# Three of four stored pairs of w_out blocks kept on chip in the ring, and the row transposes moved to the second product

## The chip, the cores and the metric

The kernel runs on one core of a Trainium2 chip. A core has TensorE (PE in the profile, with its weight loads as PEld), VectorE (DVE), ScalarE (ACT), GpSimd (POOL) and SyncE (SP), which here issues most of the DMAs. The metric is the device time of one launch in microseconds, the median of several runs.

## The reference

Attention over a window of 128 positions feeds a mixture of eight experts, and its result feeds one wide feed-forward layer:

```python
    scores = np.where(mask, scores + bias[None], -1000000000.0)
    attn = np.exp(scores - np.max(scores, axis=-1, keepdims=True)); attn = attn / (np.sum(attn, ...) + 1e-09)
    x = np.matmul(attn, v)             # (4, 8, 576, 64) -> 2304 rows of 512
    ...
    expert_idx = np.argmax(x @ w_gate, axis=1)
    for e in range(E):                 # 8 experts, w1[e] 512x1024, w2[e] 1024x512
        xe = x[expert_idx == e]
        h = np.maximum(xe @ w1[e], 0.0)
        out[mask] = gate_w[mask, None] * (h @ w2[e])
    ...
    r = np.maximum(x @ w_in, 0.0)      # w_in 512x2048
    return (r * r) @ w_out             # w_out 2048x512
```

(The softmax is drawn together here, and x is the output of the stage before in each case.)

## The kernel before

The program has three stages. Attention and the routing fill the first 183 us or so; the eight experts run from there to about 405 us; the wide layer, called moe2 here, takes the rest. Nearly all products are in float16 with each operand split into a high and a low half, so that one product is three matmuls.

**An expert.** The routed rows of expert e are fetched by row number (`gather_x`, L778) into tiles `xg`, turned by eight transposes of 128 columns each on PE (`transpose_x`, L786, into the PSUM tile `ps_d`), and copied to SBUF by ACT (L787). `turn` does this for one block of 128 rows. Expert e has two or three blocks. `s1` then computes one eighth of h per call: twelve matmuls (L795 to L797, four groups of three) into `ps_a` or `ps_b`, two buffers each, and the relu on ACT (L798, high half) and DVE (L799, low half). `s2` multiplies h by w2 into four PSUM tiles `c, c, a, b` (L849 to L851), so its fourth needs a buffer of `ps_b` that the relu of the step fc = 5 of `s1` gives back. At the end of `s2` ACT copies the result to `yT` (L854), which frees `ps_a` for the third step, fc = 2, of the next expert's `s1`.

**Weights.** Each expert has four tiles of w1 and four of w2. `load_w` brings one in two steps: SP loads 512 KB of float32 (L747) into a raw tile, and `split` writes the high half on ACT (L769) and the low half on DVE (L770) into a tile of the ring `wr`, which has 12 tiles of 128x2048 float16. Raw tiles come from the pool `rw` (four tiles) and, from expert 2 on, partly from the unused `wi` tiles.

**The wide weights.** w_in and w_out come as 64-bit words. While the experts run, `wide()` does one decoding step at a time: SP loads the words into a tile of `rw` (L866), DVE turns them into float32 in the single tile `dec` (L871, L872, L873), and when `wide()` is called the next time, the `finish` of the step splits `dec` (L918 on ACT and L919 on DVE for w_out, L902 and L903 for w_in). The list `STEPS` says after which steps of which expert it is called. The first eight steps decode the blocks of w_out called `SENT`, four pairs: they have no place on chip yet, so `finish` puts them into unused parts of four `wi` tiles, SP stores them to DRAM (`wod`, L922), and `fetch_out` brings the four pairs back into the four tiles of `rw` when moe2 begins (L960). Then come 16 steps for w_in, and eight for the blocks `KEPT`, which go to four ring tiles.

**Order.** Every engine runs its instructions in the order that a scheduler settled when the kernel was built, from the order of the code and from the buffers. A tile of the ring is given to its next user when its last reader is done, and a split for a tile not yet free waits in ACT's queue with all that stands behind it.

**moe2.** For each group G of rows and half m, `seven` makes the squared activations in a list `g` of ring tiles, two for G < 3 and four from G = 3 on; the products with w_out read the four pairs of `KEPT` and the four of `SENT`.

## Time and profile before

| | before |
|---|---|
| median of 3 runs | 749.85 us (747.07 to 750.89) |
| profiled execution | 754.0 us |
| its span, first to last instruction | 752.2 us |
| mean granted TensorE clock | 0.988 of full speed |
| PE busy | 711.6 us, 95% of the span |
| DVE busy | 594.4 us, 79% |
| ACT busy | 442.9 us, 59% |
| stores of w_out blocks to DRAM | 8 of 256 KB |
| fetches of them | 4 of 512 KB |

The profiled execution is one run; its time is its span and 1.8 us around it. The busy time of an engine is the sum of its instructions' times; the waits of PE are listed by the instruction that waited and what it waited for.

### The profile page before, as it was taken

The page shows a single profiled execution, that of the slowest core. Times are in us where ns is not written, and L with a number is a line of the kernel's source. Part 1 is how long each engine was busy: PE and PEld are TensorE (multiplying, and loading weights), DVE is VectorE, ACT ScalarE, POOL GpSimd, SP SyncE. Part 2 cuts the span into 40 slices and gives each one's busy share as a digit, 9 for nine tenths or more (in the row PEclk, how much of TensorE's full clock was granted, in tenths as well). Part 3 has the DMA queues.
Part 4 walks back from the last instruction along what each step waited for, and adds up shares of the span by engine and source line. Part 5 has one row for each costly group of instructions (what it writes and reads, how often), then busy time and mean ns, then how long its engine had stood idle before and what let it go on. Part 6 is the DMA issues. An engine that isn't in the chain of part 4 may idle for free. (4 is left out here: it accounts for less than half of the span.)

```text
span 752.2 us, 19605 instructions
## 1 busy us (share of the span) xinstructions
PE 711.6 (95%) x7979; PEld 600.8 (80%) x7979; DVE 594.4 (79%) x1454; ACT 442.9 (59%) x748; POOL 212.0 (28%) x247
## 2 busy tenths in 40 slices
PE   5989899999988999999899999999999999999996
PEld 5889799788755666788798566777899999999995
DVE  5888788864788999969987987868678787878672
ACT  5878788852466655657544342435657575757561
POOL 4493522335353401000000346533411111111011
PEclk9999999989999999999999999999999999999998
DMA  8798203765899887467713000000000000000000
GB/s 329 289 379 186 80 30 53 294 152 178 221 300 319 281 264 233 131 212 239 233 48 127 17 16 15 2 30 1 30 2 30 2 30 2 30 2 30 2 30 29
DMA packets 35656, 91.71 MB, mean 122 GB/s; under 512 B 5209, under 2 KB 13547, under 8 KB 35547
## 3 DMA queue, kind: packets, MB, share of 16 engines
q1 hardware_dynamic: 29803, 75.77, 31.6%
q0 software_dynamic: 5760, 14.65, 5.9%
q8 instruction: 64, 1.05, 0.6%
q14 instruction: 29, 0.24, 0.1%
HBM read 77.54 MB, written 13.04 MB: 120 GB/s over the span
## 5 line engine op out<-in xcount | busy, mean ns | idle before, releaser
L1178 PEld LDWEIGHTS <-wi 128*128 128x128 f16 x3024 | 170.6, 98 | 4.3 <-issue 3.1
L1315 PEld LDWEIGHTS <-wr 128*128 128x128 f16 x1008 | 98.1, 98 | 12.1 <-issue 0.7
L1201 ACT CAST wr<-work 128x1024 f16<-128x1024 f32 (+1 forms) x72 | 59.9, 832 | 58.3 <-DVE work L1207 41.6
L1178 PE MATMUL ps_a<-work,wi 128*128 128x128 f16 x1344 | 84.2, 219 | 0.0
L1178 PE MATMUL ps_b<-work,wi 128*128 128x128 f16 x1272 | 79.7, 219 | 0.4 <-ACTq L1066 0.4
L1202 DVE TENSOR_TENSOR wr<-work,wr 128x1024 f16<-128x1024 f32 (+1 forms) x72 | 70.3, 1000 | 4.4 <-ACT wr L1201 4.4
L310 PE MATMUL ps_a<-yT,wr 128*128 128x192 f32 (+2 forms) x288 | 64.9, 346 | 6.9 <-DMA wr<-in_q_dram 4.8
L322 ACT ACTIVATE pb<-pb,nm 128x192 f32<-128x192 f32 (+2 forms) x144 | 56.1, 433 | 14.8 <-DVE nm L315 14.1
L1343 POOL DMA_INDIRECT out_dram<-o,oid x18 | 25.6, 1423 | 101.4 <-ACT o L1341 66.8
L769 ACT ACTIVATE wr<-rw 128x1024 f16<-128x1024 f32 x40 | 42.2, 1057 | 19.5 <-DMA rw<-in_w_dram 18.9
L1278 POOL TENSOR_TENSOR yT<-wr 128x512 f32<-128x512 f16 x8 | 11.2, 1401 | 148.3 <-ACTq L1066 117.1
L310 PEld LDWEIGHTS ps_a<-yT,wr 128*128 128x128 f32 x288 | 45.6, 200 | 8.2 <-DMA yT<-in_k_dram 7.0
L315 DVE CUSTOM_DVE_ANT_0 pb<-ps_a,bias 128x192 f32<-128x192 f32 (+2 forms) x144 | 44.1, 326 | 9.9 <-PE ps_a L310 7.8
L770 DVE SCALAR_TENSOR_TENSOR wr<-rw,wr 128x1024 f16<-128x1024 f32 x40 | 48.8, 1220 | 3.6 <-ACT wr L769 3.4
L1210 ACT ACTIVATE work<-work 128x1024 f32<-128x1024 f32 x24 | 25.4, 1058 | 37.7 <-DVE work L1198 37.7
L333 PE MATMUL ps_b<-cst,pb 128*128 128x128 f32 x256 | 43.9, 283 | 0.7 <-ACT pts L337 0.7
L795 PE MATMUL ps_a<-work,wr 128*128 128x352 f16 (+4 forms) x112 | 33.7, 301 | 5.4 <-ACT yT L854 3.9
L778 POOL DMA_INDIRECT xg<-xd,idx x21 | 25.8, 1227 | 36.8 <-PE ps_d L786 27.7
L849 PE MATMUL ps_c<-work,wr 128*128 128x352 f16 (+5 forms) x128 | 35.9, 283 | 0.3 <-DVE work L1198 0.3
L851 PE MATMUL ps_c<-work,wr 128*128 128x352 f16 (+5 forms) x128 | 35.9, 283 | 0.0
L850 PE MATMUL ps_c<-work,wr 128*128 128x352 f16 (+5 forms) x128 | 35.9, 283 | 0.0
L1227 DVE TENSOR_TENSOR work<-work 128x512 f32<-128x512 f32 x18 | 13.0, 725 | 28.7 <-ACT work L1195 28.7
(308 smaller groups left out, 2009.5 us busy)
## 6 DMA issues: line engine op xcount, KB each, us to landing
rw<-in_w_dram SPq DMA_DIRECT2D x40, 512.0 KB
wi<-in_w_dram SPq DMA_DIRECT2D x20, 512.0 KB
rw<-in_wo_dram SPq DMA_DIRECT2D x16, 512.0 KB
rw<-in_wi_dram SPq DMA_DIRECT2D x32, 256.0 KB
wr<-in_q_dram SPq DMA_DIRECT2D x14, 512.0 KB
xd<-xhl POOLq DMA_DIRECT2D x16, 256.0 KB
yT<-in_k_dram SPq DMA_DIRECT2D x7, 576.0 KB
rw<-in_v_dram SPq DMA_DIRECT2D x12, 325.0 KB
```

The lines of the kernel that those rows point to most:

```text
L310: nc.tensor.matmul(ps[:, s, first:hi], q[g, u, hh // 4][:, hh % 4, s if u < 4 else 0, :], self.kt[g, hh // 2][:, hh % 2, key0:key0 + hi - ...
L315: self.last_ttr = nc.vector.tensor_tensor_reduce(out=pb[:, s, first:hi], in0=ps[:, s, first:hi], in1=self.bias[:, hh, first - lo:192], sca ...
L322: self.last_exp = nc.scalar.activation(pb[:, s, first:hi], pb[:, s, first:hi], AF.Exp, bias=nm[:, s:s + 1], scale=-1.0)
L333: nc.tensor.transpose(pt[:, t, :, s, :], pb[:, s, t * P:(t + 1) * P], self.idf)
L769: self.nc.scalar.activation(t[:, 0], st, AF.Copy, scale=sc)
L770: self.nc.vector.scalar_tensor_tensor(t[:, 1], st, sc, t[:, 0], op0=ALU.mult, op1=ALU.subtract)
L849: nc.tensor.matmul(py, wh, hh, start=fc == 0, stop=False)
L850: nc.tensor.matmul(py, wl, hh, start=False, stop=False)
L1178: self.nc.tensor.matmul(ps[:, j], w[:, kp, a, w0 * P:(w0 + 1) * P], v[:, 2 * x + kp], start=kp + b == 0, stop=kp == 1 and b == 2)
L1201: self.end_act = self.fin_act = nc.scalar.copy(hi, src)
L1202: self.end_dve = self.fin_dve = V.tensor_tensor(lo, src, hi, op=ALU.subtract)
L1315: nc.tensor.matmul(ps[n], x[:, v, j], y[j][:, w], start=m + i + j == 0, stop=m == 1 and i == 2 and j == 3)
```

## The change

`SENT` is cut to one pair. The other three pairs, now called `HELD`, get three ring tiles of their own when they are decoded (`wo_tiles` at the head of `out_step`), and `finish` writes straight into them. These tiles are never given back, so nine of the twelve ring tiles are left for the experts. Six of the eight stores are gone, and `fetch_out` brings one pair instead of four, so three of the four `rw` tiles are free in moe2; there the first half of each group from G = 3 on takes three of its four `g` tiles from `rw`. Independently, the transposes of the next expert's rows, which stood after the steps 3, 5 and 7 of `s1`, stand for every expert but the first inside `s2`, after its steps 1, 3 and 5, ahead of the load of a w2 tile. PE has the same instructions in number as before. In the changed file lines stand one further down up to `out_step`, four in it, and more behind it: L769 is L770, L918 is L922.

```diff
--- before.py
+++ after.py
@@ -54,7 +54,8 @@
          ((1, 3, 5, 7), (1, 3)))
 SPARE = ((), (), (4, 5, 6, 7), (4, 5, 6, 7), (4, 5, 6, 7), (6, 7), (7,), ())
 KEPT = (0, 1, 8, 9, 2, 3, 10, 11)
-SENT = (4, 5, 12, 13, 6, 7, 14, 15)
+HELD = (4, 5, 12, 13, 6, 7)
+SENT = (14, 15)
 
 C_REL, C_ID, C_LT, C_IOTA, C_J, C_TOK, C_ROWS = 0, 192, 320, 448, 457, 477, 495
 NC_CONST = 503
@@ -907,17 +908,20 @@
     def out_step(self, fc):
 
         nc = self.nc
+        if fc in HELD and fc not in self.wo_s:
+            for _ in self.wo_tiles((fc, fc + 1), lambda: self.ring(F16, [P, 2048])):
+                pass
         f = self.wide_load(self.wo, [(slice(fc * P, (fc + 1) * P), lambda r, k: r, DM, lambda st, k: st)])
 
         def finish():
-            if fc in KEPT:
+            if fc not in SENT:
                 dst = self.wo_s[fc]
             else:
                 dst = self.wi_s[4 + SENT.index(fc) % 4].rearrange("p k a c -> p (k a c)")[:, 2048:3072].rearrange(
                     "p (a d) -> p a d", a=2)
             nc.scalar.activation(dst[:, 0], f, AF.Copy, scale=WOSC)
             nc.vector.scalar_tensor_tensor(dst[:, 1], f, WOSC, dst[:, 0], op0=ALU.mult, op1=ALU.subtract)
-            if fc not in KEPT:
+            if fc in SENT:
                 o = SENT.index(fc) * 2 * DM
                 self.stored.append(lambda: nc.sync.dma_start(self.wod[:, o:o + 2 * DM],
                                                              dst.rearrange("p a d -> p (a d)")))
@@ -943,7 +947,7 @@
         self.wi_s = [wp.tile([P, 2, 2, 7 * P], F16, name=f"wi{k}", tag=f"wi{k}") for k in range(8)]
         self.wo_s, self.wo_pair = {}, {}
         self.stored, self.finish = [], None
-        self.steps = [(self.out_step, fc) for fc in SENT] + \
+        self.steps = [(self.out_step, fc) for fc in HELD + SENT] + \
             [(self.in_step, fp, kp) for fp in range(8) for kp in range(2)] + [(self.out_step, fc) for fc in KEPT]
 
     def wo_tiles(self, fcs, make):
@@ -1026,12 +1030,14 @@
                     w[1, e + 1, fc // 2] = self.load_w(1, e + 1, fc // 2)
                 if fc in STEPS[e][0]:
                     wide()
-                if fc in (3, 5, 7) and more:
+                if fc in (3, 5, 7) and e == 0:
                     turn(nxt, e + 1, fc // 2 - 1)
                 if e == 7 and fc == 1:
                     next(nrm)
 
             def then(d):
+                if more and e > 0 and d < 3:
+                    turn(nxt, e + 1, d)
                 if more:
                     w[2, e + 1, d] = self.load_w(2, e + 1, d)
                 if e + 2 < E:
@@ -1189,7 +1195,9 @@
         u, p5, z, p1 = (self.part(22528 + 2048 * k, 4 * P).rearrange("p (j n) -> p j n", j=4) for k in range(4))
         mul = lambda *a: self.product(G, m, *a)
         n = 2 if G < SG else 4
-        g = self.gts[G, m] = [self.ring(F16, [P, 2, 8 * P]) for _ in range(n)]
+        spare = 3 if n == 4 and m == 0 else 0
+        g = self.gts[G, m] = [self.ring(F16, [P, 2, 8 * P]) for _ in range(n - spare)] + \
+            [self.rw.tile([P, 2048], F16, tag="rw", name="rw").rearrange("p (a n) -> p a n", a=2) for _ in range(spare)]
 
         def keep(dst, ps):
             self.fin_act = nc.scalar.activation(dst, ps, AF.Copy, scale=RSC)
```

Three places of the order are shown, with the buffers' numbers. The first is ACT in `s1` of expert 0, where the first two decoded blocks are finished (`dec` is the decoded block, `work` the relu's result or the turned rows, `wi4` and `wi5` the old places of the blocks, `wr` a ring tile). Before:

```order
L787 COPY work_3335<-ps_d_3685 128x8x128
L918 ACTIVATE wi4_3343<-dec_3334 128x512
L817 ACTIVATE work_3335<-ps_a_3649 128x128
L817 ACTIVATE work_3335<-ps_b_3656 128x128
L817 ACTIVATE work_3335<-ps_a_3663 128x128
L817 ACTIVATE work_3335<-ps_b_3678 128x128
L918 ACTIVATE wi5_3344<-dec_3334 128x512
```

After:

```order
L788 COPY work_3335<-ps_d_3685 128x8x128
L818 ACTIVATE work_3335<-ps_a_3650 128x128
L922 ACTIVATE wr_3405<-dec_3334 128x512
L818 ACTIVATE work_3335<-ps_b_3657 128x128
L818 ACTIVATE work_3335<-ps_a_3664 128x128
L818 ACTIVATE work_3335<-ps_b_3678 128x128
L818 ACTIVATE work_3335<-ps_a_3695 128x128
L818 ACTIVATE work_3335<-ps_b_3702 128x128
L922 ACTIVATE wr_3405<-dec_3334 128x512
```

The first finish moved behind the relu of step 0 and the second behind that of step 5; before they stood ahead of step 0 and behind step 3.

The second is DVE in `s1` of expert 1, round the relu of step fc = 5, whose input is `ps_b_3994` before and `ps_b_3981` after. L770 (L771 after) with `rw` as its source is a weight split; `wr_3917` and `wr_3916` are the first tile of w1 of expert 2, `wr_3966` and `wr_3963` the second. Before:

```order
L770 SCALAR_TENSOR_TENSOR wr_3880<-rw_3878,wr_3880 128x1024
L770 SCALAR_TENSOR_TENSOR wr_3917<-rw_3915,wr_3917 128x1024
L919 SCALAR_TENSOR_TENSOR wi7_3346<-dec_3334,wi7_3346 128x512
L799 SCALAR_TENSOR_TENSOR work_3335<-ps_a_3979,work_3335 128x384
L770 SCALAR_TENSOR_TENSOR wr_3966<-wi4_3343,wr_3966 128x1024
L871 TENSOR_SCALAR dec_3334<-rw_3925 128x512
L799 SCALAR_TENSOR_TENSOR work_3335<-ps_b_3994,work_3335 128x384
```

After:

```order
L771 SCALAR_TENSOR_TENSOR wr_3879<-rw_3877,wr_3879 128x1024
L771 SCALAR_TENSOR_TENSOR wr_3916<-rw_3914,wr_3916 128x1024
L923 SCALAR_TENSOR_TENSOR wi5_3344<-dec_3334,wi5_3344 128x512
L800 SCALAR_TENSOR_TENSOR work_3335<-ps_b_3981,work_3335 128x384
L771 SCALAR_TENSOR_TENSOR wr_3963<-wi4_3343,wr_3963 128x1024
L872 TENSOR_SCALAR dec_3334<-rw_3922 128x512
L800 SCALAR_TENSOR_TENSOR work_3335<-ps_a_4014,work_3335 128x384
```

The relu of step 5 moved ahead of the split of expert 2's second tile; the split of the first tile and a finish still stand ahead of it.

The third is ACT at the end of `s2` of expert 1 and the start of `s1` of expert 2 (`yT` is the result of `s2`; the sources of the splits are raw tiles). Before:

```order
L769 ACTIVATE wr_4181<-rw_4179 128x1024
L769 ACTIVATE wr_4220<-wi7_3346 128x1024
L902 ACTIVATE wi0_3339<-dec_3334 128x896
L769 ACTIVATE wr_4303<-rw_4301 128x1024
L769 ACTIVATE wr_4337<-wi4_3343 128x1024
L854 COPY yT_75<-ps_c_4081 128x384
L854 COPY yT_75<-ps_c_4082 128x384
L854 COPY yT_75<-ps_a_4083 128x384
L854 COPY yT_75<-ps_b_4084 128x384
L769 ACTIVATE wr_4394<-rw_4392 128x1024
L798 ACTIVATE work_3335<-ps_a_4271 128x352
```

After:

```order
L770 ACTIVATE wr_4178<-rw_4176 128x1024
L788 COPY work_3335<-ps_d_4166 128x8x96
L770 ACTIVATE wr_4217<-wi7_3346 128x1024
L903 ACTIVATE wi0_3339<-dec_3334 128x896
L855 COPY yT_75<-ps_c_4048 128x384
L855 COPY yT_75<-ps_c_4049 128x384
L855 COPY yT_75<-ps_a_4050 128x384
L855 COPY yT_75<-ps_b_4051 128x384
L770 ACTIVATE wr_4300<-rw_4298 128x1024
L799 ACTIVATE work_3335<-ps_a_4268 128x352
```

The splits `wr_4303` and `wr_4337` of expert 3's first two tiles stood ahead of the copies to `yT`; now (`wr_4300` and the next) they stand behind them. The copy of the last turned block is new ahead of them, and the split of expert 2's last w2 tile (`wr_4220`, now `wr_4217`) stands ahead of them in both.

## Rows read from the trace of the kernel before

**Rows 1.** The page's first part: busy time, share of the span, instructions of each engine.

```profile
PE 711.6 (95%) x7979; PEld 600.8 (80%) x7979; DVE 594.4 (79%) x1454; ACT 442.9 (59%) x748; POOL 212.0 (28%) x247
```

**Rows 2.** Waits of PE, 155 to 405 us: what waited, for whom, total, times, longest.

```profile
PE ps_a L795 <- ACT yT L854: 3.9, 3, 2.1
PE ps_d L786 <- DMA xg<-xd,idx: 3.4, 1, 3.4
```

**Rows 3.** Stretches: length, busy of PE, PEld, DVE, ACT, POOL; PEclk, DMA share, GB/s.

```profile
208.10:211.50 3.40, 3.17 (x16) 1.96 (x17) 3.36 (x6) 2.30 (x5) 0.67 (x2) 0.50 0.96 296
242.20:245.60 3.40, 3.40 (x14) 1.72 (x13) 3.40 (x12) 3.26 (x5) 1.65 (x2) 0.50 0.74 215
...
205.00:215.00 10.00, 6.67 (x43) 4.22 (x44) 8.28 (x13) 5.83 (x8) 6.15 (x8) 0.83 0.90 295
...
356.80:378.70 21.90, 19.18 (x187) 17.09 (x187) 20.89 (x43) 12.08 (x23) 0.00 (x0) 1.00 0.70 221
378.70:413.00 34.30, 33.36 (x470) 32.55 (x468) 27.91 (x51) 14.26 (x27) 1.16 (x1) 1.00 0.24 81
...
450.00:752.20 302.20, 293.67 (x3763) 258.54 (x3760) 224.76 (x355) 166.36 (x225) 78.41 (x69) 0.99 0.05 17
```

**Rows 4.** PE in time, experts 1 to 3: start, length, line, [idle before <- releaser].

```profile
208.34 1.03 PE L786 MATMUL ps_d<-id,xg 128*128 128x128 f16 x8 [3.35 <-DMA xg<-xd,idx]
...
214.22 0.61 PE L786 MATMUL ps_d<-id,xg 128*128 128x128 f16 x8
...
218.56 0.51 PE L786 MATMUL ps_d<-id,xg 96*128 96x96 f16 x8
...
221.55 0.32 PE L849 MATMUL ps_b<-work,wr 128*128 128x384 f16 x1 [1.02 <-DVE work L799]
...
235.69 0.31 PE L795 MATMUL ps_a<-work,wr 128*128 128x352 f16 x1
...
241.55 0.31 PE L795 MATMUL ps_a<-work,wr 128*128 128x352 f16 x1 [2.12 <-ACT yT L854]
...
274.75 0.31 PE L795 MATMUL ps_a<-work,wr 128*128 128x352 f16 x1 [1.48 <-ACT yT L854]
```

**Rows 5.** DVE in time, end of s1 of expert 1.

```profile
217.86 0.68 DVE L919 SCALAR_TENSOR_TENSOR wi<-dec,wi 128x512 f16<-128x512 f32 x1
...
219.47 1.23 DVE L770 SCALAR_TENSOR_TENSOR wr<-wi,wr 128x1024 f16<-128x1024 f32 x1 [0.46 <-ACT wr L769]
...
220.95 0.55 DVE L799 SCALAR_TENSOR_TENSOR work<-ps_b,work 128x384 f16<-128x384 f32 x1
```

**Rows 6.** ACT in time, s1 of expert 0, s1 of expert 1, start of s1 of expert 2.

```profile
184.20 0.64 ACT L918 ACTIVATE wi<-dec 128x512 f16<-128x512 f32 x1
...
185.55 0.28 ACT L817 ACTIVATE work<-ps_b 128x128 f16<-128x128 f32 x1 [0.54 <-PE ps_b L816]
...
187.73 0.63 ACT L918 ACTIVATE wi<-dec 128x512 f16<-128x512 f32 x1
...
189.14 0.27 ACT L817 ACTIVATE work<-ps_b 128x128 f16<-128x128 f32 x1
...
215.62 1.06 ACT L769 ACTIVATE wr<-rw 128x1024 f16<-128x1024 f32 x1 [0.62 <-DMA rw<-in_w_dram]
...
239.33 1.04 ACT L769 ACTIVATE wr<-wi 128x1024 f16<-128x1024 f32 x1
240.28 0.84 ACT L854 COPY yT<-ps_c 128x384 f32 x2
```

**Rows 7.** SP in time: DMA issues.

```profile
209.39 0.33 SPq L747 DMA_DIRECT2D rw<-in_w_dram  x1
```

**Rows 8.** Groups of instructions, 155 to 405 us: count | busy, mean ns | idle before, releasers.

```profile
L769 ACT ACTIVATE wr<-rw 128x1024 f16<-128x1024 f32 x36 | 38.0, 1057 | 19.5 <-DMA rw<-in_w_dram 18.9 <-PE ps_b L851 0.5
L872 DVE SCALAR_TENSOR_TENSOR dec<-rw,dec 128x512 uint32<-128x512 uint32 x31 | 21.4, 689 | 0.6
L871 DVE TENSOR_SCALAR dec<-rw 128x512 uint32<-128x512 uint32 x31 | 13.4, 433 | 9.2 <-PE ps_b L851 7.9 <-DMA rw<-in_wi_dram 0.7
```

## The prediction

> **What bounds the kernel now.** I read the page's busy times first: PE is busy 95% of the span [rows 1], so what can be won is its idle time, 752.2 - 711.6 = 40.6 us in all, and stretches in which it runs at the lower clock. The change takes no matmul away, and PE executes the same instructions in another order. Next come the list of what PE waited for between 155 and 405 us, the part in which the experts run and in which all that the change removes lies: the two largest entries are three waits for the copy to `yT`, 3.9 us together, and one of 3.4 us for gathered rows [rows 2]. Then the stretches: twice the granted clock is 0.50, the 1.2 GHz level, for 3.40 us, each time just after one of those waits [rows 3]. Work that takes 3.40 us at half clock takes 1.7 us at full clock, so each such stretch costs 1.7 us beside its wait. From 450 us on PE is busy 293.67 of 302.20 us [rows 3]; there the change only puts three of four `g` tiles elsewhere, and I count that part as unchanged. So the question is what becomes of the waits in experts 1 to 7, and whether ACT and DVE, which do the splits and the decoding, give new ones.
>
> **The wait for the gathered rows.** At 208.34 us the first transposes of expert 2's rows stand in PE's queue between two steps of `s1` and the gather has not landed: 3.35 us idle [rows 4], then the half-clock stretch to 211.50 us [rows 3]. After the change the transposes stand in the next product, some 9 us later, when the rows are there. The wait goes; it costs nothing later for other experts, whose gathers caused no wait of this kind before. The three blocks themselves (1.03, 0.61 and 0.51 us, the first at half clock, so about 1.6 us on PE at full clock) are moved and not saved.
>
> But little of the 3.35 us is a gain at once, since the next thing was late too. The fourth tile of `s2` of expert 1 needs `ps_b`, free only when DVE has done the relu of step 5; PE waited 1.02 us for it, to 221.55 us [rows 4]. That relu ran at 220.95 us, behind the split of expert 2's second w1 tile at 219.47 us and, before that, a finish that ended at 217.86 + 0.68 = 218.54 us [rows 5]. In the new order it stands ahead of the second tile's split, but still behind the first tile's split and the finish. With nothing else moved it runs at 218.54 us and `ps_b` is free at 219.1 us, 2.4 us earlier than before.
>
> Two things shift that. **Earlier:** the first tile's split waited for its load; ACT began it at 215.62 us, straight after a wait for the DMA [rows 6], and the load was issued at 209.39 us [rows 7], 6.2 us before. In 205 to 215 us the DMA engines were busy 0.90 of the time at 295 GB/s [rows 3]. Three of the six removed stores were issued at 196 to 203 us; 3 x 262 KB at 295 GB/s is 2.7 us of transfer that no longer lies ahead. (The Trainium skill, "DMA: Bandwidth & Descriptors", section "Anatomy of one DMA", gives a single transfer about 2.0 us and its bytes at 436 GB/s, some 3.2 us as an estimate for 512 KB. That section measured transfers issued from GpSimd, and the 6.2 us here say that this load queued. Were it to land in 3.2 us, the split would start 3 us earlier and the forecast would be some 2 us lower, near 743.) **Later:** the decoding chain starts later. Its first finish ran at 184.20 us and now has to wait for the first ring tile of expert 0's weights, which PE reads until step 1 ends; the relu of that step began at 185.55 us, so 1.3 us. The second ran at 187.73 us and stands behind the relu of step 5 at 189.14 us, with its 0.27 us, so 1.7 us [rows 6]. Raw tiles come free at the pace of this chain, and the weight loads behind it are issued up to 1.7 us later. Between 2.7 us earlier and 1.7 us later I take 0.8 us earlier, near the middle: `ps_b` is free at about 218.3 us, 3.2 us earlier than 221.55. PE reaches it sooner and stands idle there for some 4 us, since the rest of `s1` no longer has the gather in it; I expect a half-clock stretch after it, as after the two long waits of before, 1.7 us. With the 1.6 us of transposes now behind this point, expert 2 begins 0 to 1.7 us earlier, 0.8 us in the middle.
>
> **The wait for the copy to `yT`.** Step 2 of expert 2's `s1` needs `ps_a` and began at 241.55 us after 2.12 us idle; `s1` had begun at 235.69 us [rows 4]. ACT had two weight splits ahead of the copies, the second at 239.33 us, and began the copies at 240.28 us [rows 6], 4.6 us after PE had done with `s2`. With nine ring tiles those two splits can't be that early and stand behind the copies. Then the copies start when `s2` ends, the 2.12 us go, and with them the second half-clock stretch, 1.7 us. The 1.48 us at 274.75 us [rows 4] have the same form an expert later, and I count them at a half, 0.7 us, since a finish of w_in was ahead of the copies there.
>
> **ACT and DVE after that.** Per expert the same eight splits remain, and a tile is split up to three tiles later than before. A step of `s2` is some (235.69 - 219.07) / 8 = 2.1 us from [rows 4] (the last transposes end at 219.07), one of `s1` much the same, and a tile serves two steps, so even nine tiles hold more than an expert's eight, and I take no new wait in experts 2 to 4; the bound is rival C. In experts 5 to 7 the decoding steps fall differently: by the order DVE has some 1.4 us less to do in experts 5 and 6 and some 4.8 us more in expert 7 up to the start of its `s2`: two more steps of 0.43 + 2 x 0.69 [rows 8] and a finish of 0.68 us each [rows 5], 2.5 us a step. From 378.70 to 413.00 us DVE was busy 27.91 of 34.30 us [rows 3], so 4.8 us more fill it to 95%; in 356.80 to 378.70 it was at 20.89 of 21.90, where 1.4 us less help. I take 0.5 us lost on balance, between a gain of 1 and a loss of 3.
>
> **The stores, the fetches and the ring.** Six stores and three fetches leave SP's queue. SP is far from full and the fetches lay under the start of moe2, whose DMA share is small (0.24 from 378.70 to 413.00 us, [rows 3]); beyond the 2.7 us of transfer above I count them at nothing. If that cover were thinner the loss would be on the side of before, so a gain.
>
> **The sum.** Expert 1: 0.8. `yT`: 2.1 + 1.7 + 0.7 = 4.5. Tail: -0.5. Together 4.8 us, with ends at 0 + 3.8 - 3 = 0.8 and 1.7 + 5.3 + 1 = 8. The profiled execution took 754.0 us, 4.15 over the median, so 749.2 us by its clock, and 749.2 x 749.85 / 754.0 = 745.1 at the median: **745.0 us**. About 0.5%, 3.7 us, is what a measurement of this kernel can tell from no change, so "faster" means below 746.1 and "slower" above 753.6.
>
> **The rivals.** A, the forecast: by the ends of the sum 741.9 (8 us) to 749.0 (0.8 us). For it speak the two waits with their half-clock stretches and the order of ACT and DVE, in which their causes move.
>
> B, the gain is given back: the chain is 1.7 us later all along, so `ps_b` is not free until 220.8 us and the transposes behind it push expert 2 later by 0.9 us (with the half-clock stretch 2.6), and DVE, filled in expert 7, gives back 3 us. 4.5 - 2 - 3 is about zero: 749 to 751. For it: DVE is nearly full from 356.80 us on, and the order shows the chain late. Against: the removed stores and 1.4 us less of DVE work in experts 5 and 6.
>
> C, slower: a split for a ring tile not yet free holds up ACT. ACT's splits had waited 18.9 us for raw tiles to land [rows 8], while tiles were there in time. With nine tiles the last w2 split of expert e+1 and the last turned block stand ahead of the copies to `yT`, and if the tile or its load comes late, PE waits at step 2 of every `s1` from expert 2 to 7. The copies have some 2 us of slack there: step 2 was 5.86 - 2.12 = 3.7 us after the start of `s1` without its wait, and they take about 1.6. From 0.8 us a time, six times, the 4.8 us are gone; from 1.4 us it is slower by over 0.5%. At 1.5 us, as the wait at 274.75 was, it costs 9 us: 754.0 - 4.8 + 9 = 758.2 in the profiled execution, **754 us** at the median. Against: that tile is released after step 5 of `s2`, and one split with a copy takes 2 us, as long as step 6 and 7 last. (The Trainium skill, "Perfetto Trace Analysis", section "Tensor Engine Instruction (MATMUL, LD_WEIGHTS)", calls ACT, DVE and GpSimd strict in their order while PE may pull weight loads ahead; by that rule the copies can't pass a waiting split. The trace agrees: at 240.28 us they came behind two splits though `s2` had ended 4.6 us before.)
>
> D, all of it goes: the load lands 2.7 us earlier, no half-clock stretch is left, and the later waits go too. 3.35 + 1.7 + 1.02 + 2.12 + 1.7 + 1.48 = 11.4 us, 738.5 us.
>
> **How the numbers follow.** A 0.53, B 0.27, C 0.13, D 0.07. Of A I put 0.46 below 746.1 and 0.07 above it; D is all below; B's worse end gives 0.01 to slower, the rest of it is within 0.5%: faster 0.46 + 0.07 = 0.53, same 0.07 + 0.26 = 0.33, slower 0.13 + 0.01 = 0.14. The range leaves out D and most of C: 740 to 751.5.
>
> **What would show it.** In the profile after, PE's wait for the gathered rows must be gone, and the waits of `ps_a` for the copy to `yT` must be below 1 us together; more than 4 us of them is C. At the fourth tile of expert 1's `s2` there should be a wait for DVE's relu of some 4 us with a half-clock stretch behind it; if there is none it is D. If the relu of step 5 runs after 220 us, or PE waits for DVE from 357 us on for over 2 us more than before, it is B. The stretch from 450 us to the end should be as long as before within 1 us; if not, the `g` tiles in `rw` cost something that I counted at nothing.

## The result, and the profile after

The changed kernel takes **756.06 us** (median of 5 runs, 755.55 to 760.50) against 749.50 us before (median of 5, 747.07 to 750.89): a ratio of **1.0103**, 95% interval 1.0068 to 1.0139. It is slower by 1%, where 745.0 us was forecast.

The profiled execution took 760.5 us, 4.4 over the median, much as that of before was over its own. Its first lines, to be read beside [rows 1]:

```profile
span 758.6 us, 19605 instructions
PE 711.6 (94%) x7979; PEld 600.0 (79%) x7979; DVE 594.9 (78%) x1454; ACT 443.7 (58%) x748; POOL 210.6 (28%) x247
```

No engine's work has changed by more than 1.4 us; the span is 6.4 us longer. So all of it is waiting. The waits of PE in the profile after, 155 to 420 us (what waited, for whom, total, times, longest), to be read beside [rows 2]:

```profile
PE ps_b L850 <- DVE work L800: 5.7, 3, 5.3
PE ps_b L796 <- ACT yT L855: 4.9, 1, 4.9
PE ps_a L1137 <- DVE sd L1132: 4.0, 1, 4.0
PE ps_a L796 <- DVE work L800: 2.9, 4, 1.6
PE ps_a L796 <- ACT work L788: 1.7, 1, 1.7
PE ps_c L850 <- DVE work L1206: 1.5, 1, 1.5
```

The wait for the gathered rows is gone, as meant. The six rows shown each end on DVE or ACT, none of them on a weight tile. Three of them stood in the list of before as well, but smaller: the first (1.3 us before), the third (2.3 us; `sd` is a small tile of factors by which the input of moe2 is scaled, made while experts 6 and 7 run) and the fourth (1.5 us). Stretches of the profile after (length, busy of PE, PEld, DVE, ACT, POOL; granted clock, DMA share, GB/s), to be read beside [rows 3]:

```profile
456.40:758.60 302.20, 293.71 (x3763) 258.60 (x3760) 224.57 (x355) 166.39 (x225) 76.59 (x69) 0.99 0.05 17
212.60:219.40 6.80, 4.25 (x14) 2.00 (x14) 6.70 (x11) 3.46 (x6) 4.40 (x7) 0.50 0.90 284
304.80:308.20 3.40, 3.40 (x15) 2.01 (x14) 3.20 (x5) 2.99 (x6) 0.00 (x0) 0.50 0.86 322
376.40:379.80 3.40, 2.92 (x15) 2.03 (x15) 3.40 (x6) 0.55 (x1) 0.00 (x0) 0.51 0.86 302
```

The last 302.20 us are as they were, PE busy 293.71 us against 293.67: moe2 pays nothing for the `g` tiles in `rw`. The 1.2 GHz level was granted in three stretches of the experts, 13.6 us, against 6.8 us in two.

**Where in the program.** A second trace of each kernel was taken (`before_again`, `after_again`, below). Cut at the first matmul of an expert's first product, and for the last column at the end of expert 7's second, the four traces are, in us:

| | to expert 0 | expert 0 | expert 1 | experts 2, 3 | experts 4 to 7 | the rest |
|---|---|---|---|---|---|---|
| before | 183.5 | 13.6 | 38.7 | 65.4 | 103.6 | 347.5 |
| before, second trace | 176.9 | 13.6 | 38.9 | 65.8 | 104.0 | 347.3 |
| after | 178.6 | 13.6 | 40.5 | 62.4 | 116.3 | 347.3 |
| after, second trace | 182.1 | 13.5 | 41.0 | 63.1 | 114.9 | 347.4 |

The first column, attention and routing and, from 150 us or so, the products of expert 0's first rows, is the same program in both kernels and moves by 6.6 us from one execution to the next; no difference there belongs to the change. The other columns repeat within 1.4 us. The change costs 2 us in expert 1, gains 3 in experts 2 and 3, and loses 11 to 13 in experts 4 to 7. More than half of that is lost in expert 4 alone, which takes 32.4 and 33.4 us against 25.8 and 25.7; expert 7 takes 1.8 us more in both traces. By the traces the loss is some 11 us, by the medians 6.6 us; four single executions don't settle that difference.

**The largest new wait**, 4.87 us in expert 4, followed back through the profile after, from PE to ACT, DVE and SP (start, length, line, idle before and its releaser; cut from four answers):

```profile
304.70 0.38 PE L796 MATMUL ps_b<-work,wr 128*128 128x304 f16 x1 [4.87 <-ACT yT L855]
...
303.36 0.95 ACT L903 ACTIVATE wi<-dec 128x896 f16<-128x896 f32 x1 [8.14 <-DVE dec L898]
304.21 0.43 ACT L855 COPY yT<-ps_b 128x352 f32 x1
...
299.38 0.43 DVE L872 TENSOR_SCALAR dec<-rw 128x512 uint32<-128x512 uint32 x1 [7.20 <-DMA rw<-in_wi_dram]
...
290.04 0.34 SPq L748 DMA_DIRECT2D wi<-in_w_dram  x1
290.58 0.33 SPq L748 DMA_DIRECT2D rw<-in_w_dram  x1
291.02 1.22 SPq L867 DMA_DIRECT2D rw<-in_wi_dram  x2
```

PE, in the fourth step of `s1`, needs a buffer that the copy to `yT` frees. ACT has that copy behind a finish of w_in (L903), which waited 8.14 us for the decoding. DVE began the decoding when its words landed. SP issued the load of the words at 291.02 us, behind a weight load that it could issue only at 290.04 us.

The same finish, the tenth of w_in, stood between the same copies before. There DVE had its words without a wait (ACT, DVE):

```profile
302.98 0.95 ACT L902 ACTIVATE wi<-dec 128x896 f16<-128x896 f32 x1 [2.07 <-DVE dec L897]
...
298.88 0.42 DVE L871 TENSOR_SCALAR dec<-rw 128x512 uint32<-128x512 uint32 x1
```

Counted from the start of expert 4 it began 302.98 - 301.11 = 1.9 us in, and 303.36 - 295.02 = 8.3 us in after the change. With the half-clock stretch behind it (1.7 us) this one wait is as long as what expert 4 lost.

What SP waited for, 185 to 420 us, first before and then after:

```profile
SPq L747 <- DVE wr L770: 34.4, 13, 6.6
```

```profile
SPq L748 <- DVE wr L771: 56.5, 12, 9.3
```

A weight load waits for a raw tile, and a raw tile comes free when DVE has split what is in it. The split that freed the tile for the load at 290.04 us ended at 290.02 us. It stood in DVE's order behind a whole decoding step (DVE):

```profile
284.52 0.54 DVE L872 TENSOR_SCALAR dec<-rw 128x512 uint32<-128x512 uint32 x1 [1.16 <-DMA rw<-in_wi_dram]
...
288.80 1.22 DVE L771 SCALAR_TENSOR_TENSOR wr<-wi,wr 128x1024 f16<-128x1024 f32 x1
```

So late words hold up a split, the split holds up the raw tile, and the raw tile holds up the next words. This trace shows no split that waited for PE to give a ring tile back; `e10_taken3`, below, shows four, 6.2 us together. With nine tiles the splits come later all the same: counted from the traces, the low half of a split was done on average 34 us ahead of PE's first use of the tile in expert 4 before and 27 after, and 30 and 20 us in expert 5. That the shorter lead is what starts the circle is argued and not shown. That is the reading of one place. The experiments ask whether the ring is the cause.

### The profile page after: what moved, and what is told of

It reads as the page before. It is cut to its first block, busy times and chain, and to the rows that moved or that the text cites. A ratio compares the mean times of both kernels' runs of the same rounds, so it can differ in the third digit from the quotient of the medians.

```text
span 758.6 us, 19605 instructions
## 1 busy us (share of the span) xinstructions
PE 711.6 (94%) x7979; PEld 600.0 (79%) x7979; DVE 594.9 (78%) x1454; ACT 443.7 (58%) x748; POOL 210.6 (28%) x247
## 5 line engine op out<-in xcount | busy, mean ns | idle before, releaser
L1209 ACT CAST wr<-work 128x1024 f16<-128x1024 f32 (+1 forms) x48 | 42.5, 885 | 50.3 <-DVE work L1215 42.5
L1323 PEld LDWEIGHTS <-wr 128*128 128x128 f16 x648 | 63.4, 98 | 8.2 <-issue 0.7
L1286 POOL TENSOR_TENSOR yT<-wr 128x512 f32<-128x512 f16 x10 | 14.5, 1451 | 156.0 <-DVEq L1072 119.3
L771 DVE SCALAR_TENSOR_TENSOR wr<-rw,wr 128x1024 f16<-128x1024 f32 x40 | 48.7, 1219 | 4.5 <-ACT wr L770 4.2
L1210 DVE TENSOR_TENSOR wr<-work,wr 128x1024 f16<-128x1024 f32 (+1 forms) x48 | 48.7, 1036 | 4.4 <-ACT wr L1209 4.4
L1351 POOL DMA_INDIRECT out_dram<-o,oid x18 | 23.8, 1322 | 102.1 <-ACT o L1349 67.1
L770 ACT ACTIVATE wr<-rw 128x1024 f16<-128x1024 f32 x40 | 42.3, 1060 | 15.1 <-DMA rw<-in_w_dram 13.1
L851 PEld LDWEIGHTS <-wr 128*128 128x128 f16 x288 | 28.6, 99 | 13.7 <-issue 7.0
L796 PE MATMUL ps_b<-work,wr 128*128 128x352 f16 (+4 forms) x112 | 33.3, 298 | 5.3 <-ACT yT L855 4.9
L850 PE MATMUL ps_c<-work,wr 128*128 128x352 f16 (+5 forms) x128 | 36.6, 289 | 1.5 <-DVE work L1206 1.5
L1323 PEld LDWEIGHTS <-rw 128*128 128x128 f16 x360 | 34.8, 98 | 3.8
```

Of the source, the lines that this page charges most:

```text
L770: self.nc.scalar.activation(t[:, 0], st, AF.Copy, scale=sc)
L771: self.nc.vector.scalar_tensor_tensor(t[:, 1], st, sc, t[:, 0], op0=ALU.mult, op1=ALU.subtract)
L796: nc.tensor.matmul(ph, wh, xt[:, kc], start=kc == 0, stop=False)
L850: nc.tensor.matmul(py, wh, hh, start=fc == 0, stop=False)
L1209: self.end_act = self.fin_act = nc.scalar.copy(hi, src)
L1210: self.end_dve = self.fin_dve = V.tensor_tensor(lo, src, hi, op=ALU.subtract)
```

## The experiments

Lines are those of the changed kernel where an edit starts from it, and of the kernel before where it starts from that. Ratios are against runs of the kernel before on the same chip, with 95% intervals; medians of different chips are not compared.

### The two halves of the change, and the stores

`e1_turn` keeps only the moved transposes (`HELD = ()`, `SENT` as before, no spare `g` tiles in `rw`). `e2_held` keeps only the held pairs:

```diff
-                if fc in (3, 5, 7) and e == 0:
+                if fc in (3, 5, 7) and more:
...
-                if more and e > 0 and d < 3:
-                    turn(nxt, e + 1, d)
```

`e3_held_stores` is `e2_held` with the stores back:

```diff
-            if fc in SENT:
-                o = SENT.index(fc) * 2 * DM
+            if fc not in KEPT:
+                o = (SENT + HELD).index(fc) * 2 * DM
```

Expected of `e1_turn`:

> Only the transposes are moved to the second product; all four pairs are stored and fetched as before, the ring keeps twelve tiles for the experts. Theory R (ring): the loss of the change comes from the three ring tiles, and the moved transposes alone take the wait for the gathered rows away: 745 to 749 us, and no wait of PE for the copy to yT over 2.5 us. Theory T (transposes): the turned blocks ahead of the copies to yT and in the second product cost the time: 754 to 758 us, with the large waits of the changed kernel (4.9 us for yT, 5.3 us at the fourth tile of expert 1's second product) still there.

Of `e2_held`:

> Only the three pairs are held in the ring; the transposes stand in the first product as before. Theory R: nine ring tiles make the splits, the release of raw tiles and with them the weight loads in SP's queue later, and the words to be decoded stand behind those loads: 755 to 760 us, with the wait for the gathered rows back (3.4 us) and SP waiting over 50 us for the low halves of splits. Theory T: 745 to 750 us.

Of `e3_held_stores`:

> As e2_held, and the three held pairs are also stored to DRAM by six stores of 256 KB that nobody reads. If the removed stores were worth what the prediction gave them (2.7 us of transfer ahead of the weight loads) this is 1 to 3 us slower than e2_held; if they were hidden anyway it is within 1 us of it. Theories R and T do not differ here.

Measured: `e1_turn` 750.15 us, ratio 1.0025 (1.0000 to 1.0049); `e2_held` 755.01 us, 1.0080 (1.0052 to 1.0108); `e3_held_stores` 755.73 us, 1.0108 (1.0081 to 1.0135). The loss is that of the held pairs, and the transposes alone are level or a little worse, not the gain that theory R gave them. The waits of PE in `e1_turn`, 155 to 420 us:

```profile
PE ps_a L850 <- DVE work L800: 3.7, 1, 3.7
PE ps_a L796 <- DVE work L800: 2.9, 6, 0.8
PE ps_a L1137 <- DVE sd L1132: 2.3, 1, 2.3
PE ps_b L850 <- DVE work L800: 1.7, 1, 1.7
...
PE ps_a L796 <- ACT yT L855: 0.4, 1, 0.4
```

The gathered rows and most of the copy to `yT` are gone from the list, 6.9 us of [rows 2], and 3.7 + 1.7 us stand at the start of expert 1's second product, for relus. The six stores made a difference of 0.3%, their intervals overlap, and the medians, of one chip, are 0.7 us apart; the stores' worth isn't told apart from nothing. One sign failed: SP was to wait over 50 us for the low halves of splits in `e2_held`, and the row (185 to 420 us, as above) is 41.8 us, the same as in `e1_turn`, which loses next to nothing.

### Is it the ring, or the late start of the decoding?

In the changed kernel the first finish also waits for a ring tile, and the whole decoding runs later. The first two finishes ran 2.1 and 5.8 us after the start of expert 0 instead of 0.7 and 4.3. `e4_held1` holds one pair, the first decoded; `e8_held_last` holds one pair, the last decoded; both leave the transposes in the first product. The edit of `e8_held_last`, cut:

```diff
-HELD = (4, 5, 12, 13, 6, 7)
-SENT = (14, 15)
+HELD = (14, 15)
+SENT = (4, 5, 12, 13, 6, 7)
...
-        self.steps = [(self.out_step, fc) for fc in HELD + SENT] + \
+        self.steps = [(self.out_step, fc) for fc in SENT + HELD] + \
```

`e9_taken1` and `e10_taken3` are the kernel before with one and three ring tiles that GpSimd writes in expert 0 and reads in expert 7, and nothing else:

```diff
+                if e == 0 and fc == 2:
+                    taken = [self.ring(F16, [P, 2048]) for _ in range(3)]
+                    for t in taken:
+                        nc.gpsimd.memset(t[:, :1], 0.0)
```

`e13_held3_last` is `e2_held` with the stored pair decoded first.

Of `e4_held1`:

> One pair is held instead of three (eleven ring tiles for the experts, six stores and three fetches left), transposes in the first product as before. Theory R, with a loss that grows as tiles are taken: 750 to 754 us, between before and e2_held. Theory T: 748 to 750 us, as before.

Of `e8_held_last`:

> One pair is held, as in e4_held1, but the last of the four to be decoded instead of the first, so that the first finishes of the decoding need no ring tile and the chain starts as early as before; six stores and three fetches are left, transposes in the first product. Theory S (late start): e4_held1 lost 7 us because its first finish waits for a ring tile and the whole decoding runs 1.3 to 1.7 us late: then this is 748 to 751 us. Theory R (ring): eleven tiles are too few whenever they are taken: 754 to 757 us, as e4_held1.

Of `e9_taken1`:

> The kernel before, with one ring tile taken out of use from expert 0 to expert 7 (GpSimd writes one column of it at the start and reads it at the end); all stores, fetches, transposes and the decoding as before. Theory R: 753 to 757 us. Theory S: within 2 us of before, 748 to 751 us.

Of `e10_taken3`:

> As e9_taken1 with three ring tiles taken out. Theory R: 754 to 758 us, not much over one tile, as e2_held with three was not over e4_held1 with one. Theory S: within 3 us of before, up to 752 us.

Of `e13_held3_last`:

> Three pairs are held, but the pair that is stored and fetched is decoded first and the held ones after it, so that the first two finishes need no ring tile; transposes in the first product. It stands to e2_held as e8_held_last to e4_held1. Theory S (late start) gives 749 to 752 us; theory R (nine tiles are too few) 754 to 758 us, as e2_held.

Measured: `e4_held1` 1.0102 (1.0074 to 1.0130), `e8_held_last` 0.9987 (0.9956 to 1.0018), `e9_taken1` 1.0059 (1.0025 to 1.0093), `e10_taken3` 1.0115 (1.0051 to 1.0179), `e13_held3_last` 1.0129 (1.0088 to 1.0170). Three tiles taken out of the kernel before, with its stores, its transposes and its start of the decoding left alone, cost as much as the whole change: theory R holds for three tiles, and starting the decoding early (`e13_held3_last`) doesn't mend it. For one tile the runs disagree. The two with one pair held fit theory S: decoded first it costs 1%, more than either theory gave it, decoded last nothing. But `e9_taken1`, at 753.72 us, fits theory R: one tile taken early costs 0.6% though the decoding starts as before. The largest waits of PE in `e10_taken3`, 155 to 420 us, are of the kind of the profile after, in a kernel whose wait for gathered rows is still there. Here ACT's splits did wait for PE to give a ring tile back, four times, 6.2 us together against 1.2 before:

```profile
PE ps_a L795 <- DVE work L799: 6.0, 4, 2.6
PE ps_a L795 <- ACT yT L854: 5.5, 3, 4.7
PE ps_d L786 <- DMA xg<-xd,idx: 2.4, 1, 2.4
```

### The queue of SP, and where the tiles are missed

The words of w_in stand behind waiting weight loads. `e11_words_pool` (from the changed kernel) and `e12_before_words_pool` (from before) load them from GpSimd's queue:

```diff
-            nc.sync.dma_start(dst(st, k), c0(r, k))
+            (nc.gpsimd if len(pieces) > 1 else nc.sync).dma_start(dst(st, k), c0(r, k))
```

Of `e11_words_pool`:

> The changed kernel, with the words of w_in to be decoded loaded from GpSimd's queue instead of SyncE's, so that they no longer stand behind weight loads that wait for a raw tile. Theory Q (queue): the large waits of the changed kernel behind a late decoding (4.9 us for the copy to yT in expert 4, 4.0 us in expert 6) come from that order in SyncE's queue: 748 to 752 us. Theory L (late splits): with nine tiles the splits and the raw tiles themselves are late, and the words are not what matters: 754 to 758 us, with waits of PE for relus behind splits that wait for their load.

Of `e12_before_words_pool`:

> The kernel before with the same edit of the queue. Theory Q: the twelve tiles hide the order, so 747 to 751 us, as before. Theory L: the same. A gain of over 3 us would say that the order in SyncE's queue costs time in the kernel before as well; a loss, that descriptors written by GpSimd cost time of their own, by which e11_words_pool has to be read.

Measured: 1.0294 (1.0254 to 1.0335) and 1.0299 (1.0254 to 1.0344). Both theories missed, and the pair is inconclusive on the queue, since it made a wait of its own. In `e12_before_words_pool` PE waited 21.9 us once for a relu, and DVE stood in front of that relu for words whose load had GpSimd's own DMAs ahead of it, the lists of rows and the gathers (DVE, GpSimd in time):

```profile
238.47 0.43 DVE L872 TENSOR_SCALAR dec<-rw 128x512 uint32<-128x512 uint32 x1 [21.24 <-DMA rw<-in_wi_dram]
...
233.84 1.50 POOL L867 DMA_DIRECT2D rw<-in_wi_dram  x2
```

`e14_words_first` leaves the queue and changes the order in it: `wide()` is written ahead of `load_w` at both places, which puts the words of the wait above ahead of both loads that they stood behind. `e17_before_words_first` does it to the kernel before. `e18_taken3_late` is `e10_taken3` with the tiles taken from expert 4 on (`if e == 4 and fc == 2`).

Of `e14_words_first`:

> The changed kernel, with the decoding step written ahead of the weight load at every place where both stand, so that the loads of the words to be decoded stand up to two weight loads earlier in SyncE's queue (the one that came late in expert 4 stands ahead of the two that it stood behind). Theory Q (the words are late because they stand behind weight loads that wait for a raw tile): the wait of 4.9 us for the copy to yT in expert 4 goes, with its half-clock stretch, 4 to 7 us less than the changed kernel. Theory L (the splits themselves are late with nine tiles, wherever the words stand): within 2 us of the changed kernel.

Of `e17_before_words_first`:

> The kernel before with the same edit. Theory Q: with twelve tiles the loads seldom wait and the place of the words matters little, within 2 us of before. A gain as large as that of e14_words_first over the changed kernel would say that the edit helps for a reason that has nothing to do with the ring.

Of `e18_taken3_late`:

> The kernel before, with three ring tiles taken out of use as in e10_taken3 but only from expert 4 on. Theory L: the loss comes where fewer raw tiles are left (experts 5 and 6), where the lead of the splits can't be built up again: 4 to 8 us over before. Theory E (early): the tiles are missed in experts 0 to 3, where stores, words and weights share SyncE's queue: within 2 us of before.

Measured: `e14_words_first` 1.0059 (1.0022 to 1.0097), `e17_before_words_first` 1.0042 (1.0020 to 1.0064), `e18_taken3_late` 1.0088 (1.0056 to 1.0120). In `e14_words_first` the place in question is clean (SP, ACT):

```profile
286.17 1.21 SPq L867 DMA_DIRECT2D rw<-in_wi_dram  x2
288.96 0.34 SPq L748 DMA_DIRECT2D wi<-in_w_dram  x1
...
296.50 0.81 ACT L855 COPY yT<-ps_c 128x352 f32 x2
297.19 0.47 ACT L855 COPY yT<-ps_a 128x352 f32 x1
297.54 0.48 ACT L855 COPY yT<-ps_b 128x352 f32 x1
```

The words were issued ahead of the waiting load, the four copies follow one another, and the wait of 4.9 us isn't there: expert 4 takes 26.4 us, about as before. The same edit makes the kernel before slower, so it is no general gain. But it takes back less than half, 3.3 us by the ratios, between the two forecasts: the medians' intervals, 1.0059 here and 1.0103 for the changed kernel, overlap, and in the traces experts 4 to 7 take 111.8 us against 115 to 116 and 104 before. What is lost now stands in expert 5, 27.4 us against 23 to 24 in the traces after, and in the same circle (DVE, SP, ACT, PE):

```profile
321.19 0.43 DVE L872 TENSOR_SCALAR dec<-rw 128x512 uint32<-128x512 uint32 x1 [5.10 <-DMA rw<-in_wi_dram]
327.42 0.34 SPq L748 DMA_DIRECT2D wi<-in_w_dram  x1
332.03 1.06 ACT L770 ACTIVATE wr<-wi 128x1024 f16<-128x1024 f32 x1 [3.23 <-DMA wi<-in_w_dram]
334.73 0.27 PE L796 MATMUL ps_a<-work,wr 128*128 128x256 f16 x1 [2.06 <-DVE work L800]
```

DVE waited for words, its split came late behind their decoding, SP could issue the next weight load only at 327.42 us, and the split of that load stood ahead of the relu that PE needed. Theory Q explains the wait in expert 4. Whether the rest is the late splits themselves (theory L) this run doesn't show, since the edit didn't bring all the words in time. In `e18_taken3_late` PE waits as late as in the profile after, in the same chain, at 357 us (ACT, start of expert 6):

```profile
353.57 1.06 ACT L769 ACTIVATE wr<-wi 128x1024 f16<-128x1024 f32 x1 [3.16 <-DMA wi<-in_w_dram]
354.53 0.63 ACT L854 COPY yT<-ps_c 128x256 f32 x2
356.54 0.95 ACT L902 ACTIVATE wi<-dec 128x896 f16<-128x896 f32 x1 [1.38 <-DVE dec L897]
357.40 0.35 ACT L854 COPY yT<-ps_a 128x256 f32 x1
```

A split that waited 3.16 us for its load and a finish that waited 1.38 us stand ahead of the copy. By the medians the tiles taken from expert 4 on cost most of what they cost when taken from the start (1.0088 and 1.0115); by the traces, experts 4 to 7 take 109.0 us against 116.1, less than half. The two differ in experts 4 and 5 (25.7 and 21.9 us here, 30.1 and 23.9 there) and are alike in 6 and 7 (29.9 and 31.6, 30.5 and 31.6).

### How many tiles, and a version that is slightly faster

`e16_held_last_turn`, `e19_held2_last_turn` and `e20_held3_last_turn` are the whole change, transposes too, with the last one, two and three of the four pairs held (eleven, ten and nine tiles for the experts).

Of `e16_held_last_turn`:

> The whole change cut to one pair, and to the pair that is decoded last: six stores and three fetches left, eleven ring tiles from expert 1 on, transposes in the second product. e8_held_last without the transposes was level with before (0.9987), and the transposes alone cost 1.3 us (1.0025): if the two add up, 0 to 2 us over before, 749 to 752 us. If the transposes profit from one pair held, below before by over 2 us; if the change is bad for any ring tile taken, 754 us or more.

Of `e19_held2_last_turn`:

> As e16_held_last_turn with the last two of the four pairs held: ten ring tiles from expert 1 on, four stores and two fetches left, transposes in the second product. If the lead of the splits is what counts and is used up tile by tile, this lies between e16_held_last_turn (0.997 of before) and the changed kernel (1.010): 750 to 754 us. If eleven tiles are enough and nine are not because of a step between them, it is at one of the two ends.

Of `e20_held3_last_turn`:

> The whole change, with the one pair that is stored decoded first and the three held ones after it. If nine tiles in experts 4 to 6 cause the loss, the early start of the decoding does not help, 756 to 760 us as the changed kernel; if the late start of the decoding is a large part, 750 to 753 us.

Measured: 0.9968 (0.9945 to 0.9992), 1.0116 (1.0083 to 1.0148), 1.0065 (1.0040 to 1.0090). With one pair held, decoded last, the change is **faster than before** by 0.3%, 749.40 us against 752.51 us on that chip; the interval ends just short of 1. With two it costs as much as the whole change, and three are not worse than two: here the cost comes in one step, between eleven and ten tiles. The stages of the traces, in us, cut as above, with the ring tiles left for the experts and the time that DVE waited for words of w_in, 185 to 420 us:

| | tiles | ratio | expert 1 | experts 2, 3 | experts 4 to 7 | wait for words |
|---|---|---|---|---|---|---|
| before (two traces) | 12 | 1 | 38.7, 38.9 | 65.4, 65.8 | 103.6, 104.0 | 0.7, 0.8 |
| `e1_turn` | 12 | 1.0025 | 41.8 | 60.6 | 106.3 | 1.3 |
| `e17_before_words_first` | 12 | 1.0042 | 37.3 | 65.5 | 106.9 | 0.7 |
| `e8_held_last` | 11 | 0.9987 | 40.6 | 59.8 | 107.6 | 2.9 |
| `e16_held_last_turn` | 11 | 0.9968 | 39.8 | 59.8 | 104.3 | 2.9 |
| `e4_held1` | 11 | 1.0102 | 40.2 | 67.2 | 107.6 | 2.6 |
| `e9_taken1` | 11 | 1.0059 | 39.1 | 65.0 | 109.3 | 3.9 |
| `e18_taken3_late` | 9, from expert 4 | 1.0088 | 39.4 | 67.6 | 109.0 | 4.5 |
| `e19_held2_last_turn` | 10 | 1.0116 | 36.9 | 62.0 | 115.7 | 11.0 |
| `e2_held` | 9 | 1.0080 | 37.2 | 61.2 | 113.4 | 7.8 |
| `e3_held_stores` | 9 | 1.0108 | 39.7 | 61.6 | 113.4 | 8.7 |
| `e10_taken3` | 9 | 1.0115 | 38.6 | 62.7 | 116.1 | 13.9 |
| `e13_held3_last` | 9 | 1.0129 | 34.5 | 66.1 | 117.7 | 16.9 |
| `e14_words_first` | 9 | 1.0059 | 38.5 | 62.7 | 111.8 | 9.7 |
| `e20_held3_last_turn` | 9 | 1.0065 | 38.0 | 61.5 | 112.9 | 12.4 |
| the change (two traces) | 9 | 1.0103 | 40.5, 41.0 | 62.4, 63.1 | 116.3, 114.9 | 14.8, 12.5 |

Every kernel with nine or ten tiles from an early expert on loses 8 to 14 us in experts 4 to 7; those with eleven or twelve lose 0.5 to 5.5. The last column parts them in the same way, 7.8 us and more against 3.9 and less, though it doesn't explain what `e4_held1` and `e9_taken1` lose. SP's wait for the low halves of splits doesn't: it is 48.1 us in `e8_held_last`, level with before, and 41.8 in `e2_held`, which loses 0.8%. In experts 2 and 3 most kernels with a part of the change gain 3 to 6 us, whichever half they have; `e4_held1`, with its late start, `e9_taken1` and `e13_held3_last` don't, and the last gains 4 us in expert 1 instead. `e16_held_last_turn` has that gain and nearly keeps the time of experts 4 to 7. The waits of PE over 0.6 us in it, 155 to 420 us:

```profile
PE ps_b L796 <- DVE work L800: 4.6, 1, 4.6
PE ps_a L796 <- DVE work L800: 2.8, 3, 2.1
PE ps_b L1137 <- DVE sd L1132: 0.8, 1, 0.8
PE ps_a L817 <- ACT work L809: 0.8, 1, 0.8
```

Neither the gathered rows nor the copy to `yT` is in the list any more.

### The two second traces

> The kernel before a second time, for a second trace: the waits that are the same in both traces (the gathered rows, the copy to yT) belong to the kernel, those that differ by over 1 us to the run. Both theories expect 747 to 754 us; the stage of attention, 183.5 us in the first trace up to expert 0, should be 3 to 5 us shorter, as in the other traces.

> The changed kernel a second time, for a second trace: waits that come in both belong to the kernel. 755 to 760 us. By theories R and Q the waits of PE in experts 4 to 6 (4.9 us for yT, 1.8 us for a turned block, 4.0 us for the scaling) come again, if not at the same places; a trace without them would put them down to the run.

`before_again` ran in 748.25 us, `after_again` in 763.47 us, one run each. The second trace of before has the wait for the gathered rows (2.7 us) and the same three for `yT` (3.9 us); the second trace of after has the wait of 4.7 us for `yT` at the same step of expert 4, 4.0 us at the fourth tile of expert 1's second product and 1.3 us for a turned block. They belong to the kernels; the length of attention does not. Two things did not repeat: the wait for the scaling (`sd`) was 2.0 us instead of 4.0, and 1.1 us for gathered rows stood in the second trace of after.

## Why the prediction was wrong

**The wait for the gathered rows: it went, as said, and the next thing was late, as said; the size was off.** PE stood 5.26 us at the fourth tile where some 4 us were forecast, in the profile after:

```profile
215.15 0.48 PE L850 MATMUL ps_b<-work,wr 128*128 128x384 f16 x1 [5.26 <-DVE work L800]
```

Counted from the start of expert 1, `ps_b` came free 215.15 - 192.11 = 23.0 us in, and before 221.55 - 197.02 = 24.5 us [rows 4]: 1.5 us earlier, not 3.2. The relu ran at 214.54 us straight behind the two splits and the finish that the order shows ahead of it. And the half-clock stretch was 6.8 us, not 3.4; it began 2.55 us before the wait ended, and PE was busy 4.25 us of it, so it cost about 2.1 us instead of 1.7. So expert 1 lost 2 us where 0.8 was to be gained. One term held: the first two finishes came 1.35 and 1.56 us later, where 1.3 and 1.7 were taken. `e1_turn` shows the same with all stores in place, so the removed stores didn't decide it; the 2.7 us of transfer that I counted for them is not shown by `e3_held_stores` either.

**The wait for the copy to `yT`: right in kind, smaller in size.** 4.5 us were forecast from experts 2 and 3; they take 2.7 to 3.0 us less in the traces after, and 5 to 6 less in `e1_turn` and `e8_held_last`.

**"ACT and DVE after that": here the prediction failed.** It said that nine tiles hold more than an expert's eight, and took no new wait in experts 2 to 4 and 0.5 us for the tail; measured were 11 to 13 us. The step counted the tiles that PE needs, and PE indeed never waits for a weight tile. It left out what follows when a split comes later: the raw tile that it empties, SP's next load, behind that the words, the decoding and the next finish, and behind the finish in ACT's and DVE's order the copies to `yT` and the relus. What the runs showed in its place is the wait of DVE for words, 0.7 us before and 14.8 after (`e10_taken3`: 13.9), and the finish that it makes late, for which ACT waited 8.14 us in expert 4 where it had waited 2.07. The waits of DVE for words, 185 to 420 us, before and then after:

```profile
DVE dec L871 <- DMA rw<-in_wi_dram: 0.7, 2, 0.5
```

```profile
DVE dec L872 <- DMA rw<-in_wi_dram: 14.8, 5, 7.2
```

How nine tiles bring it about was followed in expert 4 and, in `e14_words_first`, in expert 5; the rest of the way stays argued.

**Rival C had the right kind of mechanism and nearly the right time**, 754 us, at a chance of 0.13. Its place was another: it had a split hold up ACT, and in the profile after a finish did, waiting for the decoding. Its price was spread wrongly (six waits of 1.5 us, where there were a few of 2 to 5 us, two of them in experts 4 and 6 with a half-clock stretch of 1.7 us at most). The reason given against it, that the tile is released after step 5, was a reason against one link alone. What the Trainium skill says of ACT and DVE being strict in their order ("Perfetto Trace Analysis", section "Tensor Engine Instruction (MATMUL, LD_WEIGHTS)") is what the profile after shows: the copy at 304.21 us came directly behind a finish that had kept ACT idle for 8.14 us.

**Rival B** (the decoding starts late) may be real for one pair: `e4_held1` against `e8_held_last`, 7.4 us of it in experts 2 and 3. But the two also differ in when the tile is taken, and `e9_taken1` lost 0.6% without a late start. For three pairs `e2_held` against `e13_held3_last` doesn't show it, and the whole change against `e20_held3_last_turn` (1.0103 and 1.0065, intervals that overlap) leaves it open.

**moe2: right**, unchanged within 0.2 us.

**Open.** Why the cost comes in one step between eleven and ten tiles in the last three kernels, while one and three tiles taken from the kernel before cost 0.6% and 1.2%; the order of the instructions changes with each kernel, and no run holds it fixed while the number of tiles changes. And how much of the loss is SP's order and how much the splits: in the one pair of kernels that asks, the words were still late in expert 5.

## What to carry to other kernels

A buffer ring that is long enough for its reader can still be too short for its writer: ask who stands behind the instruction that waits for a free buffer, on its own engine, and through the buffer that it empties on the queue that fills it. Then check the row that you suspect in a kernel that did not lose: here the waits of the DMA queue grew in such kernels too, and the wait of DVE for its words hardly did. And when a wait is removed, as the gathered rows here, the gain is the distance to the next late thing, less the half-clock stretch that may stand behind that one's wait.

## What the runs showed of the hardware

The granted clock was 0.50, the 1.2 GHz level, for 3.4 us in some cases and 6.8 us in others round the end of single waits of PE of 2.1 to 5.3 us: 6.8 us with 5.26 us of idle in the profile after, 3.4 us with 4.87 us, and 3.4 us with 2.12 us in that of before. By the page of the profile after, loads of 512 KB took a median of 5.4 us from issue to landing into `rw` and 6.8 us into `wi`, and the words issued at 291.02 us let DVE begin only at 299.38 us. Attention, the same code in all kernels, took with routing and expert 0's first rows from 176.9 to 183.5 us, more than most of the differences studied here: single traces of this kernel are compared by stage, not by span.
